# A new order of tasks and choice of engines for an adaLN block with linear attention

## The chip, the cores and the metric

The kernel runs on one core of a Trainium2 chip. The metric is the device time of one execution in microseconds (us); lower is better. Times quoted from the profile belong to one profiled execution of the kernel before the change. Its engines are called by short names: PE multiplies matrices, DVE, ACT and POOL work on vectors, and SP only issues DMAs.

## The reference

One transformer block over a sequence of 2048 tokens of width 512, in bfloat16. A vector `c` gives six vectors of scale, shift and gate. The attention is linear: queries and keys go through a small matrix per head (32 heads of 16), and two softmaxes (of the result and of its negative) make a feature map of 32.

```python
mod = (silu(c) @ w_mod).reshape(6, 512)          # sa, ca, ga, sb, cb, gb
h = layernorm(x) * (1 + ca) + sa
q, k, v = h @ wqkv                               # 32 heads x 16
phi_q = concat(softmax(q @ w_phi), softmax(-q @ w_phi))
phi_k = concat(softmax(k @ w_phi), softmax(-k @ w_phi))
kv, z = sum_s(phi_k[s] v[s]), sum_s(phi_k[s])    # over all 2048 tokens
x = x + ga * ((phi_q @ kv) / (phi_q @ z + 1e-6)) @ wo
h = layernorm(x) * (1 + cb) + sb
x = x + gb * ((sigmoid(h @ w_gate) * (h @ w_up)) @ w_down)      # width 1376
```

## The kernel before

The tokens are cut into 16 tiles of 128, and each step on a tile (or on a piece of one) is a *task*: a name, the engines that can do it, a function that issues its instructions, the tasks it depends on and the buffers it uses. A table `ORDER` (lines 39 to 91), one long text of task names, sets everything else. `arrange` walks it once:

```python
for word in text.split():
    name, _, e = word.partition("@")
    t = self.tasks[name]
    t.eng = LETTER[e] if e else next(iter(t.alts))
    assert t.eng in t.alts and t.deps <= done and t not in done, name
    for b in t.bufs:
        if b.slot is None:
            b.slot = slots[b.cls].pop(0)
```

So a name's place in the table sets its place in its engine's program (each engine runs its instructions in order), a suffix `@A`, `@D` or `@P` puts it on ACT, DVE or POOL, and buffers are handed out in the table's order from a fixed number per class; the one that became free first is taken first. Exponentials, feature maps and the like share a class of seven. A task waits by semaphore for its inputs and for the last readers of the buffer that it takes over. Nothing else is scheduled.

The first stage runs until the key-value sum is complete:

- `ld_*` on SP load 256-KB pieces of x (`x0b` is tiles 2-3, `x0a` tiles 0-1, L537), the key weights (`wk0`, `wk1`, L545), the scale and shift weights (`wm00a` to `wm01b`, four pieces, L542), then the value weights (L551), the gate's and the second block's modulation weights (`wmga`, L555; `wmm2`, 1.5 MB, L556), `wo` (L557) and the MLP's weights. DMA transposes on the same queue serve query weights (L669) and tiles 10 to 13 (`xT1`, L736).
- `st1` (L702, L703), `rs1` (POOL L712, L713 or ACT L709, L710), `nmr1` (L718) and `xn1` (L731) are the first layer norm; PE transposes the tiles (`tph`, L744) and `hm1` (L753 on DVE and POOL, L751 on ACT) applies scale and shift, which `modc1` on PE (L630) and `modc1c` (ACT L635, L636 or DVE L638) have put into columns.
- PE: folding of `w_phi` into the weights, then `K` (L817), `V` (L821), `Q` (L871). `warm` (L600) are 18 filler matmuls at the beginning.
- Per tile: `e` and `qe`, exponentials on ACT (L776); `n` and `qn`, sums on DVE (L780); `r`, reciprocals (DVE L798 or ACT L794, L795); `phi` of keys (L787) and `qphi` of queries (L784), the products exponential by reciprocal, on DVE or POOL:

```python
engine(e).tensor_tensor(ph[:, a * P:b * P].rearrange(...), ee[:, a:b].rearrange(...), kr[:, a:b]..., op=ALU.mult)
...
port=("POOL", "DVE"))
```

  A tile's feature map may be cut into halves or quarters (`phi13.0` and `phi13.4`; `phi11.0` to `phi11.6`).
- `kv` on PE (L282) adds every tile's feature map times values; `kvn` and `kvz` on DVE (L294, L299) mask the sum into `kvb`.

Behind it PE does `num` (L326, queries by `kvb`), `out` (L356), and the MLP (`g`, `u` at L447, `y` at L485), with DVE, ACT and POOL serving it. `wo` (L851) and `wd` (L860) on POOL multiply the gates into the weights.

Of the kernel before, what the change touches and what calls it, by code (L numbers as in the profile page):

```python
# [15 lines left out]
P = 128  # L16
S, D, H, DH, F = 2048, 512, 32, 16, 1376
# [23 lines left out]
nmr1_1 nmr1_2 ld_x1b st1_6 st1_7 tpw1 tpw3 wTc3 wTc1 tpw2 fold10 foldc10 wTc2 ld_wm00b ld_x1a ld_wm00a tph00 fold11 fold13 rs1_4 foldc13 fold12 foldc12 xn1_3  # L41
xn1_2 xn1_1 modc1.0 tph10 tph11 st1_4 tph20 tph01 ld_x2b foldc11 tph22 warm1_5 modc1c0 hm1_11@A nmr1_4 xn1_6 xn1_7 st1_5 rs1_3@P st1_11 st1_10 warm1_6
hm1_20@A hm1_10@A tph21 warm1_7 tph41 tph42 hm1_21 rs1_6@P nmr1_3 tph13 ld_wm01a ld_wm01b modc1.1 hm1_01@A hm1_00@A hm1_41@A tph03 tph23 K2a ld_x2a tph02
modc1c1 st1_8 ld_x3a warm1_8 K1a hm1_23 xn1_5 xn1_4 tph12 nmr1_6 st1_9 hm1_03@A hm1_13@A hm1_02@A ld_wv0 wqT3 xn1_10 xn1_11 rs1_5@P K0a K0b tph31 hm1_42@A
warm1_9 hm1_12@A hm1_22@A tph32 e0.0 K3a tph30 K3b hm1_30@A ld_wmga K1b tph33 warm1_10 tph40 st1_14 st1_15 st1_13 hm1_31@A hm1_32 wqT0 e3.0 wqT1 K2b hm1_40
nmr1_5 rs1_8@P n0.0 nmr1_8 hm1_33 e2.0 V0a V1a fold03 xn1_9 xn1_8 V1b V0b e1.0 n2.0 V2a V2b tph50 hm1_50 warm1_11 xn1_15 xn1_14 n1.0 V3a wqT2 fold00 fold01
tph43 r0.0@A va1 va0 phi0.0 foldc03 fold02 foldc01 foldc02 n3.0 st1_12 foldc00 xT1_10 xT1_11 r2.0 va2@D ld_wmm2 modca.0 modca.1 hm1_60@P hm1_63@P hm1_62@P
tph82 hm1_82@A r3.0@A modcac r1.0@A phi2.0@D phi1.0@D V3b K4a K4b rs1_7@P Q0 Q2 kv0.0 Q1 qe0.0 va3 qe2.0 hm1_43@A qe1.0 modc2.0 tph52 modc2.1 tph51 nmr1_7
xn1_12 xn1_13 phi3.0@D ld_wo qn0.0 modc2c e4.0 kv1.0 qn2.0 hm1_52 kv2.0 Q4 K5a kv3.0 xT1_12 xT1_13 qphi0.0@P qphi0.1@P qn1.0 qe4.0 qphi2.1 tph80 K5b hm1_80@A
hm1_51@A e5.0 pT0 qphi2.0 n4.0 r4.0@A qn4.0 n5.0 phi4.0@D qphi1.1@P hm1_61@P qphi1.0@P tph53 V5 K7a V4 va5 hm1_53@A V6 pT2 hm1_70@P qphi4.1 va4 hm1_71 mask4  # L50
va6 K6a K7b K6b e6.0 K8 tph83 hm1_83 r5.0 qphi4.0@P e8.0 pT1 pT4 ld_wd2 tph81 hm1_81 n6.0 n8.0 e7.0 n7.0 V7 kv4.0 hm1_72@P K11 K9 V9 K14 V8 r6.0@A e9.0 va7
va9 r7.0@A e11.2 e11.6 phi5.0 phi6.0 hm1_73@P n9.0 r9.0@A kv5.0 gwa gra gwb e11.4 e14.0 K10 phi7.0@D kv6.0 K12 V10 kv7.0 e14.4 r8.0 n11.6 n11.2 r11.6 phi9.0
e10.0 e12.0 ld_wd ld_wu0 grb n11.4 n14.0 r11.2 n14.4 r14.0 n10.0 r14.4@A phi8.0 va8 V11 V14 n12.0 e11.0 K13 n11.0 phi11.6 r11.4 wo1 r11.0 va10 r10.0@A va11
kv8.0 kv9.0 phi11.2@D phi11.0@D phi10.0@D phi11.4@D V12 K15 e13.0 wmod_free ld_wg0 phi14.4 phi14.0 kv10.0 kv11.4 kv11.6 Q6 kv11.0 e13.4 r12.0@A e15.4 n13.0
n13.4 r13.0 r13.4 n15.4 e15.0 va14 V15 V13 qe6.0 va12 kv11.2 n15.0 r15.0 r15.4@A va13 phi13.4 Q5 phi15.4 phi13.0@D va15 phi15.0@D phi12.0@D wo0 wo3 Q3 kv12.0
# [4 lines left out]
hm0.4 hm0.9 u0.2 u0.0 num6a tg0.5 tg0.0 rd3a u3a u0.5 g0.2 hm0.0 hm0.5 rd6a nmr2_1 qe10.0 tg0.2 oT4 g0.10 u0.10 wd6 hm0.2 g0.3 pT7 tg0.3 u6a g0.6 num6b u0.3  # L60
y0.0 y0.1 rd6b tg0.10 hm0.10 hm0.3 num5a num5b u6b rd5b wd3 wd4 wd5 oT3 oT6 xn2_1 qe13.0 tg0.6 rd5a y0.2 u5b g0.7 tg0.7 out4 u5a oT5 qn11.0 u0.6 u0.7 xnT1
num7a hm0.6 hm0.7 mod13@A mod12@A rd7a x1_4 y0.3 out3 qphi11.1@P qphi11.0@P x1_3 st2_3 out6 mod10@A mod11@A g1.2 tg1.2 g1.1 tg1.1 num7b wd7 u1.3 u1.2 hm1.2
u7a g1.4 u1.1 y0.4 rd7b hm1.1 u1.4 y0.5 tg1.4 hm1.4 g1.0 g1.10 u1.10 g1.3 u7b st2_2 rs2_2 tg1.10 tg1.3 hm1.10 hm1.3 pT11 out5 tg1.0 u1.7 g1.7 x1_6 nmr2_2 u1.0
hm1.0 g1.5 u1.5 x1_5 qn10.0 wd8 y0.6 g1.6 oT7 xn2_2 xn2_3 g1.8 y0.7 Q14 y0.8 wd10 tg1.7 tg1.5 hm1.5 out7 u1.8 u1.6 st2_4 tg1.6 xnT2 xnT3 wd9 x1_7 qphi10.0 Q12
hm1.7 st2_6 mod21@P mod20@P qphi10.1@P y1.0 pT10 tg1.8 mod22@A mod23@A hm1.6 g1.9 y1.1 y1.2 tg1.9 u1.9 y0.9 y1.3 y1.4 g2.5 y0.10 g2.6 st2_5 qe12.0 st2_7 hm1.8
qn9.0 tg2.5 qe14.0 rs2_4 hm1.9 rs2_3 nmr2_4 y1.5 u2.0 g2.1 g2.0 tg2.0 xn2_7@D hm2.0 nmr2_3 fin0 y1.6 g2.2 tg2.2 u2.6 u2.2 hm2.2 u2.1 num11b y1.7 g2.4 rd11b
u11b xn2_6@P xnT7 xnT6 u2.5 tg2.1 xn2_5 qphi9.1@P hm2.1 tg2.6 u2.8 xn2_4 hm2.5 g2.3 num11a rd11a u11a u2.9 qphi9.0@P xnT5 y1.8 xnT4 tg2.4 u2.4 hm2.4 hm2.6
# [991 lines left out]
```

## Time and profile before

| | before |
|---|---|
| median of 3 runs | 205.57 us (205.29 to 205.62) |
| profiled execution: span | 203.3 us |
| what lies around the span, against the median | 2.27 us |
| PE busy | 194.9 us (96%) |
| DVE busy | 160.6 us (79%) |
| ACT busy | 105.9 us (52%) |
| POOL busy | 102.1 us (50%) |
| DMA | 22.94 MB in 49,453 packets |

The profile gives no time of its own for the profiled execution but its span. Busy shares are means over two very different stages: until about 58 us all of PE, DVE, ACT and POOL work, and behind that PE is the busiest by far. An engine's busy time counts its fillers too (PE's `warm`). Idle time of an engine is listed with what released it.

### The profile page before, as it was taken

To read this page: it belongs to the slowest core of one execution; us is meant where nothing else is said; L and a number is where in the kernel's file an instruction comes from. 1 tells how busy PE (TensorE), PEld (TensorE's weight loads), DVE (VectorE), ACT (ScalarE), POOL (GpSimd) and SP (SyncE) were. 2 spreads that over 40 slices of the span, in tenths; PEclk is the share of its full clock that TensorE was granted. 3 is DMA by queue.
4 is the path that set the end of the run, shared out by engine and by line. 5 is a ranking of instruction groups with operands and counts; after the bars stand their busy time and mean duration, and the time that the engine had idled before them with its cause. 6 is when DMAs were issued, how large, how long until landed. Compare 5 with 4: busy or idle time off the path is not lost.

```text
span 203.3 us, 4138 instructions
## 1 busy us (share of the span) xinstructions
PE 194.9 (96%) x1447; PEld 106.7 (52%) x1471; DVE 160.6 (79%) x374; ACT 105.9 (52%) x257; POOL 102.1 (50%) x143
## 2 busy tenths in 40 slices
PE   7789999999999999999999999999999999999993
PEld 2455655555464687668844444444444444444442
DVE  3899999999999999999897797794969844326633
ACT  2799999999978984556451115212113311324100
POOL 4698977789689999767670056230030324000000
PEclk9999999999999999999999999999999999999999
DMA  5999975669952792417637224433112030100111
GB/s 172 331 329 182 233 264 102 123 82 280 400 213 43 146 102 55 94 37 106 125 59 103 51 54 103 101 83 77 26 26 69 13 79 31 40 13 7 50 55 55
DMA packets 49453, 22.94 MB, mean 113 GB/s; under 512 B 38065, under 2 KB 47634, under 8 KB 49426
## 3 DMA queue, kind: packets, MB, share of 16 engines
q1 hardware_dynamic: 48896, 22.59, 48.6%
q8 instruction: 13, 0.21, 0.4%
q14 instruction: 14, 0.11, 0.2%
q10 hardware_dynamic: 530, 0.02, 0.1%
HBM read 11.58 MB, written 2.10 MB: 67 GB/s over the span
## 4 chain that ended last, share of the span: by engine, by line
PE 75%; DVE 8%; ACT 4%; DMA 4%; issue 4%; POOL 3%; SPq 0%; POOLq 0%; DVEq 0%
PE y_ps L485 19%; PE u_ps L447 18%; PE g_ps L447 17%; PE a_ps L356 5%; DMA wmod_sb<-in_w_mod_dram 4%; PE k_ps L817 3%; PE warm L600 3%; DVE ks L780 3%; PE num L326 2%; POOL phi L787 2%; PE q_ps L871 2%; PE v_ps L821 2%; PE g_ps L449 1%; ACT h1T L751 1%; DVE qks L780 1%
## 5 line engine op out<-in xcount | busy, mean ns | idle before, releaser
L457 ACT ACTIVATE tg<-g_ps 128x512 bf16<-128x512 f32 (+5 forms) x66 | 28.8, 455 | 66.7 <-PE g_ps L447 39.5
L468 DVE SCALAR_TENSOR_TENSOR wmod_sb<-tg,u_ps 128x512 bf16<-128x512 bf16 (+4 forms) x63 | 30.3, 492 | 18.0 <-ACT tg L457 11.3
L485 PE MATMUL y_ps<-wd_sb,wmod_sb 128*128 128x512 bf16 (+4 forms) x180 | 44.2, 366 | 0.2
L447 PEld LDWEIGHTS <-wg_sb 128*128 128x128 bf16 (+1 forms) x252 | 21.9, 99 | 16.1 <-issue 0.2
L447 PEld LDWEIGHTS <-wu_sb 128*128 128x128 bf16 (+1 forms) x252 | 21.8, 99 | 16.0 <-issue 0.3
L784 POOL TENSOR_TENSOR qphi<-qe,qks 128x512 bf16<-128x512 bf16 x24 | 25.1, 1063 | 3.9 <-DMA pT<-qphi 1.0
L485 PEld LDWEIGHTS <-wmod_sb 128*128 128x128 bf16 (+1 forms) x187 | 17.1, 98 | 16.0 <-issue 0.6
L447 PE MATMUL u_ps<-wT_sb,wu_sb 128*128 128x512 bf16 (+2 forms) x124 | 23.8, 322 | 0.1
L447 PE MATMUL g_ps<-wT_sb,wg_sb 128*128 128x512 bf16 (+2 forms) x122 | 23.0, 321 | 0.2
L447 PE MATMUL g_ps<-wqk_sb,wg_sb 128*128 128x128 bf16 (+4 forms) x127 | 19.9, 286 | 0.1
L447 PE MATMUL u_ps<-wqk_sb,wu_sb 128*128 128x128 bf16 (+4 forms) x127 | 19.8, 286 | 0.2
L492 DVE TENSOR_TENSOR ot<-y_ps,x 128x512 bf16<-128x512 f32 (+2 forms) x17 | 11.1, 654 | 10.5 <-PE y_ps L485 10.4
L780 DVE TENSOR_REDUCE qks<-qe 128x64 bf16<-128x1024 bf16 x16 | 19.2, 1204 | 0.0
L780 DVE TENSOR_REDUCE ks<-e 128x64 f32<-128x1024 bf16 (+2 forms) x22 | 19.1, 905 | 0.0
L376 POOL TENSOR_SCALAR ve<-mv 128x2 f32<-128x2 f32 (+1 forms) x8 | 1.8, 226 | 34.2 <-DVE mv L366 34.1
L776 ACT ACTIVATE e<-k_ps 128x512 bf16<-128x512 f32 (+2 forms) x44 | 17.7, 504 | 0.1
L776 ACT ACTIVATE qe<-q_ps 128x512 bf16<-128x512 f32 x32 | 17.3, 608 | 0.8 <-POOL phi L787 0.4
L787 POOL TENSOR_TENSOR phi<-e,kr 128x1024 bf16<-128x1024 bf16 (+2 forms) x10 | 14.5, 1454 | 3.9 <-ACT kr L795 2.1
L817 PE MATMUL k_ps<-wqk_f,h1T 128*128 128x512 bf16 x61 | 15.9, 379 | 0.1
L356 PE MATMUL a_ps<-wo_sb,oT 128*128 128x512 bf16 x60 | 15.9, 379 | 0.2
L871 PE MATMUL q_ps<-wqk_f,h1T 128*128 128x512 bf16 x60 | 15.7, 379 | 0.2
L821 PE MATMUL v_ps<-wv_sb,h1T 128*128 128x512 bf16 x62 | 15.5, 379 | 0.0
(131 smaller groups left out, 306.4 us busy)
## 6 DMA issues: line engine op xcount, KB each, us to landing
out_dram<-ot SPq DMA_DIRECT2D x15, 128.0 KB, 1.8
x_sb<-in_A_x_dram SPq DMA_DIRECT2D x6, 256.0 KB, 4.9
wmod_sb<-in_w_mod_dram SPq DMA_DIRECT2D x1, 1536.0 KB, 7.4
wu_sb<-in_B_w_up_dram SPq DMA_DIRECT2D x1, 1376.0 KB, 11.0
wg_sb<-in_B_w_gate_dram SPq DMA_DIRECT2D x1, 1376.0 KB, 10.4
wd_sb<-in_B_w_down_dram SPq DMA_DIRECT2D x1, 1280.0 KB, 8.0
wmod_sb<-in_w_mod_dram SPq DMA_DIRECT2D x4, 256.0 KB, 6.0
wqk_sb<-in_A_wqkv_dram SPq DMA_DIRECT2D x2, 256.0 KB, 4.5
```

The lines of the kernel that those rows point to most:

```text
L356: pe.matmul(ap_[:], lhsT=oT[:, j, :], rhs=wo_sb[:, j, :], start=(j == 0), stop=(j == KT - 1))
L447: pe.matmul(ps[:fsz, 0:n], lhsT=w[:, j, ft * P:ft * P + fsz], rhs=h[:, j, 0:n], start=(j == 0), stop=(j == KT - 1))
L457: G.add(f"tg{k}.{ft}", {"ACT": 0.13 + n * 0.00083}, lambda e, tg=tg, g_ps=g_ps, fsz=fsz, n=n: act.activation(tg[:fsz, 0:n], g_ps[:fsz, 0:n ...
L468: dve.scalar_tensor_tensor(hm_all[:fsz, hm[k].slot, ft, 0:n], tg[:fsz, 0:n], 1.0, u_ps[:fsz, 0:n], op0=ALU.add, op1=ALU.mult)
L485: mm = pe.matmul(y[:, 0:c1 - c0], lhsT=hm_all[:fsz, hm[k].slot, ft, tl * P:(tl + 1) * P], rhs=wd_sb[:fsz, ft, c0:c1], start=(ft == 0), sto ...
L776: act.activation(ee[:, a:b, s].rearrange("p g f h -> p g (f h)"), kp[:, a * 64:b * 64].rearrange("p (g n) -> p g n", n=64), ACT.Exp, scale ...
L780: dve.tensor_reduce(ks[:, a:b].rearrange("p g s h -> p (g s) h"), ee[:, a:b].rearrange("p g s f h -> p (g s) h f"), axis=AX.X, op=ALU.add)
L784: engine(e).tensor_tensor(ph[:].rearrange("p (g s f h) -> p g s f h", s=2, f=DH, h=4)[:, :, s], ee[:, :, s], ks[:, :, 1 - s].unsqueeze(2). ...
L787: engine(e).tensor_tensor(ph[:, a * P:b * P].rearrange("p (g f h) -> p g f h", f=DH, h=4), ee[:, a:b].rearrange("p g s f h -> p (g s) f h" ...
L817: pe.matmul(kp[:], lhsT=h1T[:, j, t * P:(t + 1) * P], rhs=wqk_f[:, j, D:2 * D], start=(j == 0), stop=(j == KT - 1))
L821: pe.matmul(vp[:], lhsT=h1T[:, j, t * P:(t + 1) * P], rhs=wv_sb[:, j, :], start=(j == 0), stop=(j == KT - 1))
L871: pe.matmul(qp[:], lhsT=h1T[:, j, t * P:(t + 1) * P], rhs=wqk_f[:, j, 0:D], start=(j == 0), stop=(j == KT - 1))
```

## The change

Only the table `ORDER` is replaced. All task names stay; their order and some engine suffixes change. A line or two of it:

```diff
-pmem ld_x0b wdz warm0 c1 warm1_0 warm1_1 bd st1_2 st1_3 warm1_2 warm1_3 c2 rs1_2 ld_x0a ld_wk0 warm1_4 tpw0 st1_0 rs1_0 wTc0 st1_1 ld_wk1 rs1_1 c3 xn1_0
+wdz warm0 c1 warm1_0 warm1_1 ld_x0b mask4 ld_wk0 c2 ld_x0a st1_3 tpw0 warm1_2 tpw1 wTc0 warm1_3 ld_wk1 warm1_4 warm1_5 warm1_6 wTc1 st1_2 rs1_2 warm1_7 pmem
...
```

On SP, at the program's beginning before the change (L537 are x tiles, L545 key weights, L542 scale and shift weights; two rows alike in a row are counted):

```order
L537 DMA x_sb<-in_A_x_dram 128x2x512 x2
L545 DMA wqk_sb<-in_A_wqkv_dram 128x2x512 x2
L537 DMA x_sb<-in_A_x_dram 128x2x512
L542 DMA wmod_sb<-in_w_mod_dram 128x4x256
L537 DMA x_sb<-in_A_x_dram 128x2x512
L542 DMA wmod_sb<-in_w_mod_dram 128x4x256
L537 DMA x_sb<-in_A_x_dram 128x2x512
L542 DMA wmod_sb<-in_w_mod_dram 128x4x256 x2
L537 DMA x_sb<-in_A_x_dram 128x2x512
```

The same place of SP after it:

```order
L537 DMA x_sb<-in_A_x_dram 128x2x512
L545 DMA wqk_sb<-in_A_wqkv_dram 128x2x512
L537 DMA x_sb<-in_A_x_dram 128x2x512
L545 DMA wqk_sb<-in_A_wqkv_dram 128x2x512
L542 DMA wmod_sb<-in_w_mod_dram 128x4x256
L537 DMA x_sb<-in_A_x_dram 128x2x512
L542 DMA wmod_sb<-in_w_mod_dram 128x4x256
L537 DMA x_sb<-in_A_x_dram 128x2x512
L542 DMA wmod_sb<-in_w_mod_dram 128x4x256 x2
L537 DMA x_sb<-in_A_x_dram 128x2x512
```

The first half of the key weights now stands between the first two loads of x, and the last two of the scale and shift weights stand ahead of the first load of the third pair of x tiles (tiles 8 and 9). Later on SP, the two transposes of tiles 10 and 11 (L736) stood ahead of the 1.5 MB of modulation weights (L556) and `wo` (L557), and stand behind them now.

On POOL, from phi5.0 (the first row; `phi` is L787) to the `wo` pieces behind the last feature map of the first stage (phi15.4), before:

```order
L787 TENSOR_TENSOR phi<-e,kr 128x1024 x2
L753 TENSOR_SCALAR h1T<-h1T,modc 128x256
L787 TENSOR_TENSOR phi<-e,kr 128x1024 x2
L787 TENSOR_TENSOR phi<-e,kr 128x256
L851 TENSOR_TENSOR wo_sb<-wo_sb,ga_sb 128x512
L787 TENSOR_TENSOR phi<-e,kr 128x512 x4
L851 TENSOR_TENSOR wo_sb<-wo_sb,ga_sb 128x512 x3
```

And the same place of POOL after:

```order
L787 TENSOR_TENSOR phi<-e,kr 128x1024
L753 TENSOR_SCALAR h1T<-h1T,modc 128x256
L851 TENSOR_TENSOR wo_sb<-wo_sb,ga_sb 128x512
L787 TENSOR_TENSOR phi<-e,kr 128x1024 x3
L787 TENSOR_TENSOR phi<-e,kr 128x256 x4
L851 TENSOR_TENSOR wo_sb<-wo_sb,ga_sb 128x512
L787 TENSOR_TENSOR phi<-e,kr 128x512 x4
L851 TENSOR_TENSOR wo_sb<-wo_sb,ga_sb 128x512 x2
```

POOL gets all four quarters of tile 11 instead of one, and one more `wo` piece ahead of the four halves of tiles 13, 14 and 15.

On DVE, from the reciprocals of tile 11 to the mask of the key-value sum (`kvb`), before:

```order
L798 RECIPROCAL kr<-ks 128x16 x2
L787 TENSOR_TENSOR phi<-e,kr 128x256 x2
L787 TENSOR_TENSOR phi<-e,kr 128x1024
L787 TENSOR_TENSOR phi<-e,kr 128x256
L780 TENSOR_REDUCE ks<-e 128x32 x2
L798 RECIPROCAL kr<-ks 128x32 x2
L780 TENSOR_REDUCE ks<-e 128x32 x2
L798 RECIPROCAL kr<-ks 128x32
L787 TENSOR_TENSOR phi<-e,kr 128x512 x2
L787 TENSOR_TENSOR phi<-e,kr 128x1024
L780 TENSOR_REDUCE qks<-qe 128x64
L294 TENSOR_TENSOR kvb<-kvacc_595,mask_77 128x16x16
```

The end of the same stretch after (its earlier part is `n` and `r` in another order, without the three quarters of tile 11):

```order
L787 TENSOR_TENSOR phi<-e,kr 128x1024
L780 TENSOR_REDUCE ks<-e 128x32
L798 RECIPROCAL kr<-ks 128x64
L798 RECIPROCAL kr<-ks 128x32
L780 TENSOR_REDUCE ks<-e 128x32
L787 TENSOR_TENSOR phi<-e,kr 128x1024
L780 TENSOR_REDUCE ks<-e 128x32 x2
L798 RECIPROCAL kr<-ks 128x32 x3
L787 TENSOR_TENSOR phi<-e,kr 128x512 x2
L780 TENSOR_REDUCE qks<-qe 128x64
L299 SCALAR_TENSOR_TENSOR kvb<-kvacc_685,mask_77 128x16
L294 TENSOR_TENSOR kvb<-kvacc_685,mask_77 128x16x16
```

DVE has the reciprocals of tile 12 and of the second half of tile 15 from ACT, and no longer the three quarters of tile 11. Further ahead (not shown), the mask's own reduction (L591) moves from the place behind a `qphi` in the middle of the stage to the second instruction of DVE, four `hm1` leave DVE and one of half size comes to it, two modulation columns (L638) come to it from ACT, and two rsqrt pairs (`rs1_4` from ACT, and `rs1_7` from further back) stand ahead of phi0.0 on POOL. Behind `kvb` the order of the MLP's pieces changes throughout; the work of the last tile pair ends the program as before.

More of the change, by code (lines that the diff above doesn't have):

```diff
@@ L44 @@
[L44 to L55, printed above, removed]
@@ L60 @@
[L60 to L67, printed above, removed]
@@ new lines @@
+r3.0@A modc2.1 nmr1_7 xn1_13 xT1_13 hm1_60@P modc2c Q0 phi2.0@D kv0.0 hm1_62@P xn1_12 xT1_12 phi1.0@D qn4.0 kv1.0 qe0.0 qe1.0 hm1_80@A kv2.0 V6 Q2 phi3.0@D
+qn0.0 qphi4.1@P va6 kv3.0 qphi4.0@P qn1.0 qe2.0 pT4 qphi0.0 qphi0.1@P hm1_63@P e4.0 K7a qphi1.0@P hm1_70@P qphi1.1 hm1_61@P qn2.0 K6a tph81 K7b qphi2.0@P K6b
+V8 n4.0 e5.0 va8 hm1_73@P V4 n5.0 hm1_71@P e6.0 pT0 pT1 K9 r4.0@A va4 V5 va5 K8 qphi2.1 r5.0 K11 phi4.0@D kv4.0 V7 phi5.0 hm1_72@P n6.0 e7.0 pT2 e9.0 wo1 e8.0
+hm1_81@A e11.4 K10 n7.0 va7 e11.6 n9.0 kv5.0 r6.0 V9 r9.0 n8.0 K14 r7.0@A phi7.0@D V11 phi6.0 e11.0 n11.0 n11.6 e11.2 n11.2 n11.4 K13 kv6.0 kv7.0 r8.0 phi9.0
@@ L87 @@
+y14.9 fin12 y14.10 fin14 y15.4 st12 st14 y15.5 y15.6 y13.4 y13.5 y13.6 y13.7 y13.8 y13.9 y13.10 fin13 st13 y15.7 y15.8 y15.9 y15.10 fin15 y15.0b y15.1b st15
+y15.2b y15.3b y15.4b y15.5b y15.6b y15.7b y15.8b y15.9b y15.10b fin15b st15b
 """
```

66 lines of the change are left out of this document (40 added, 26 removed).

## The prediction

> **What bounds the kernel now.** I first read the busy time of each engine in five stretches of the span (columns: stretch, its length, then busy us and instructions of PE, PEld, DVE, ACT and POOL, the granted clock, the DMA share and GB/s).
>
> ```profile
> core 0: us, PE busy (x) PEld busy (x) DVE busy (x) ACT busy (x) POOL busy (x), PEclk, DMA share, GB/s
> 0.00:10.00 10.00, 7.47 (x46) 3.53 (x47) 6.12 (x21) 5.36 (x13) 5.22 (x23) 1.00 0.85 250
> 10.00:20.00 10.00, 9.23 (x89) 5.29 (x90) 9.45 (x32) 9.86 (x28) 9.07 (x17) 1.00 1.26 256
> 20.00:57.90 37.90, 37.36 (x355) 21.02 (x360) 37.05 (x67) 36.47 (x103) 30.43 (x32) 1.00 0.83 222
> 57.90:103.40 45.50, 44.62 (x465) 32.01 (x469) 42.76 (x119) 31.60 (x77) 38.43 (x45) 1.00 0.50 86
> 103.40:203.30 99.90, 96.17 (x502) 44.87 (x510) 65.25 (x140) 22.65 (x39) 19.00 (x30) 1.00 0.25 55
> ```
>
> Behind 57.9 us PE alone is dense: 140.8 of 145.4 us. Ahead of it PE is busy too, but part of that is warming and its real work is not what ends the stage: PE, DVE and ACT are all nearly full from 20 to 57.9 us, and POOL is the one with air, 7.5 us idle of 37.9. What ends the stage is seen at its last step, in the timeline of POOL, DVE and PE around 57 us (start, length, engine, line, operation, tiles, idle time before it and its releaser).
>
> ```profile
> 56.48 1.20 POOL L787 TENSOR_TENSOR phi<-e,kr 128x512 bf16<-128x512 bf16 x1 [1.23 <-ACT kr L795]
> 55.47 1.29 DVE L787 TENSOR_TENSOR phi<-e,kr 128x512 bf16<-128x512 bf16 x3
> 57.87 0.43 DVE L294 TENSOR_TENSOR kvb<-kvacc,mask 128x256 bf16<-128x256 f32 x1
> 58.57 0.80 PE L326 MATMUL num<-kvb,pT 128*128 128x68 bf16 x20 [0.36 <-DVE kvb L299]
> ```
>
> The key-value sum needs the feature map `phi` of every one of the 16 token tiles. POOL's last one (phi15.4) ends at 57.68, PE adds it, DVE masks the sum at 57.87 (`kvb`), and PE starts `num` at 58.57 after waiting. So kvb is a gate between two stages: whatever moves it moves everything behind, because behind it PE has nearly no slack to give back (0.9 us in the first 45.5). The question is when kvb comes in the new order, and both DVE and POOL must be through their lists for it.
>
> **The change, step 1: DVE's head.** DVE's waits up to 58 us are few (waiting instruction, what it waited for, total us, times, longest).
>
> ```profile
> DVE st L702 <- DMA x_sb<-in_A_x_dram: 2.4, 1, 2.4
> DVE h1T L753 <- PE tp_h L744: 0.6, 2, 0.4
> DVE phi L787 <- POOL h1T L753: 0.3, 1, 0.3
> DVE nmr L718 <- ACT rs L710: 0.3, 1, 0.3
> ```
>
> SP now issues x tiles 2-3, half the key weights, then x tiles 0-1; before, both x pairs went first. The issues of those loads today, with the time to landing of each, and the statistics of the first tile of the second pair:
>
> ```profile
> x_sb<-in_A_x_dram SPq DMA_DIRECT2D x1, 256.0 KB, 2.8
> x_sb<-in_A_x_dram SPq DMA_DIRECT2D x1, 256.0 KB, 3.1
> wqk_sb<-in_A_wqkv_dram SPq DMA_DIRECT2D x1, 256.0 KB, 4.4
> 5.21 0.66 DVE L702 BATCH_NORM_STATS2 st<-x_sb 128x6 f32<-128x512 bf16 x1
> ```
>
> They are issued about 0.5 us apart (0.9, 1.5 and 2.0 us in the trace); the third lands at about 6.3. If x tiles 0-1 take the third place they land there, and DVE, ready for them at 5.21, waits 1.1 us. The other end is no wait at all, if place does not matter and this load keeps 3.1 us. I take 1.1, because queue and size are those of the third row. Against it: the mask reduction (0.28 us, L591) moves from a full place at 38 us into DVE's first wait, where it is free (-0.28); the `nmr` wait (0.3) and the two `h1T` waits (0.6) can go, as their instructions stand further back now. Head together: 1.1 - 0.28 - 0.9 = about -0.1.
>
> The last two scale-and-shift loads (L542) move ahead of the first load of tiles 8-11, so they come one place of 256 KB earlier, and those tiles one place later. What the former release, the last columns of scale and shift, comes from PE, and PE's list ahead of `num` holds the same amount of real work as before and does not set the gate; the statistics of tiles 8-11 stand behind others in DVE's list. I cost this at nothing; its cover is DVE and ACT, 9.45 and 9.86 us busy of the 10 from 10 to 20 us. Without that cover it is worth at most a place in the queue, about 0.5 us by the distance of the issues, either way.
>
> **Step 2: DVE's list up to phi7.0.** Mean durations by shape up to 57.8 us (count | busy us, mean ns):
>
> ```profile
> L787 DVE TENSOR_TENSOR phi<-e,kr 128x1024 bf16<-128x1024 bf16 x7 | 4.7, 682 | 0.3 <-POOL h1T L753 0.3
> L753 DVE TENSOR_SCALAR h1T<-tp_h,modc 128x256 bf16<-128x256 bf16 x9 | 3.5, 393 | 0.6 <-PE tp_h L744 0.6
> L798 DVE RECIPROCAL kr<-ks 128x64 bf16<-128x64 f32 x3 | 1.6, 538 | 0.0
> L784 DVE TENSOR_TENSOR qphi<-qe,qks 128x512 bf16<-128x512 bf16 x3 | 1.4, 478 | 0.0
> L798 DVE RECIPROCAL kr<-ks 128x16 bf16<-128x16 f32 x4 | 0.9, 234 | 0.0
> L787 DVE TENSOR_TENSOR phi<-e,kr 128x512 bf16<-128x512 bf16 x2 | 0.7, 388 | 0.0
> 44.58 0.69 DVE L787 TENSOR_TENSOR phi<-e,kr 128x1024 bf16<-128x1024 bf16 x1 [0.29 <-POOL h1T L753]
> ```
>
> Ahead of the phi of tile 7 DVE loses four `hm1` (1.57) and gains one of half size (0.39 at most), loses two `qphi` and gains two, gains two reciprocals (1.08) and two small modulation columns (0.23 each at most, the shortest reciprocal). Net +0.3 at most; I take +0.2. phi7.0 ends at 45.27 today, so at 45.27 + 0.2 - 0.1 = about 45.4.
>
> **Step 3: POOL behind phi7.0.** POOL's timeline of today from there on, and its mean durations by shape from 18 to 57.8 us:
>
> ```profile
> 45.42 4.61 POOL L787 TENSOR_TENSOR phi<-e,kr 128x1024 bf16<-128x1024 bf16 x3 [0.87 <-ACT kr L795]
> 49.99 1.17 POOL L851 TENSOR_TENSOR wo_sb<-wo_sb,ga_sb 128x512 bf16<-128x512 bf16 x1
> 52.19 3.06 POOL L787 TENSOR_TENSOR phi<-e,kr 128x512 bf16<-128x512 bf16 x3 [1.03 <-DVE phi L787]
> ```
>
> ```profile
> L787 POOL TENSOR_TENSOR phi<-e,kr 128x1024 bf16<-128x1024 bf16 x5 | 9.6, 1917 | 1.6 <-ACT kr L795 0.9 <-PE kvacc L282 0.5
> L851 POOL TENSOR_TENSOR wo_sb<-wo_sb,ga_sb 128x512 bf16<-128x512 bf16 x2 | 2.3, 1164 | 0.0
> L787 POOL TENSOR_TENSOR phi<-e,kr 128x256 bf16<-128x256 bf16 x1 | 0.6, 619 | 0.1
> ```
>
> Today POOL starts phi9.0 at 45.42 and ends phi15.4 at 57.68: 12.3 us, of which 2.3 are the two waits shown. In the new table phi9.0 writes into the buffer that phi7.0 has read out, so it starts just behind it again, at about 45.5. From there to phi15.4 POOL now has two phi of 1.92, four quarters of tile 11 at 0.62 (three of them were DVE's), one `wo` piece of 1.16 and four halves of 1.02: 3.8 + 2.5 + 1.2 + 4.1 = 11.6, less a little overlap at the seams: 11.5 us without a wait. DVE in return loses three of those short phi (under 0.39 each, the mean of a half tile) and a reciprocal and gets two that ACT had (0.54 each at most): even. POOL gets to phi9.0 in time: from phi0.0 to there it loses two `qphi` and gains two, and gains one `hm1` (1.64 us for three today, shown below) and one `wo` piece, 1.7 us net, out of 7.5 - 2.3 = 5.2 us of idle time; another rsqrt pair now comes ahead of phi0.0.
>
> **Step 4: DVE and POOL at the same time.** In the trace a two-operand product of DVE out of SBUF hardly ever runs beside one of POOL: POOL mostly waits just then. In the few places where they meet, this is what it costs (two qphi of DVE, the first beside POOL's second, which ends at 33.05; then a qphi of POOL beside one of DVE's that ends at 38.10, and one alone).
>
> ```profile
> 30.98 2.07 POOL L784 TENSOR_TENSOR qphi<-qe,qks 128x512 bf16<-128x512 bf16 x2 [0.55 <-PE kvacc L282]
> 32.73 0.60 DVE L784 TENSOR_TENSOR qphi<-qe,qks 128x512 bf16<-128x512 bf16 x1
> 33.25 0.41 DVE L784 TENSOR_TENSOR qphi<-qe,qks 128x512 bf16<-128x512 bf16 x1
> 37.68 0.42 DVE L784 TENSOR_TENSOR qphi<-qe,qks 128x512 bf16<-128x512 bf16 x1
> 37.79 1.22 POOL L784 TENSOR_TENSOR qphi<-qe,qks 128x512 bf16<-128x512 bf16 x1 [0.82 <-DVE phi L787]
> 35.37 1.06 POOL L784 TENSOR_TENSOR qphi<-qe,qks 128x512 bf16<-128x512 bf16 x1
> ```
>
> DVE lost 0.19 us of 0.32 us side by side, POOL 0.16 of 0.31, and phi15.4 above 0.15 (1.20 against 1.05) of 0.28: about half of the time they share. With POOL dense in the new order the gaps are gone. Behind phi7.0 DVE has two phi of 0.68 and two of 0.39, 2.1 us; if three quarters of that lie beside POOL's work, half of it is 0.8 us on POOL. Ahead of phi7.0 DVE's products come in five groups; five times 0.16 by three quarters is 0.6 us on DVE. [...]
>
> [...]
>
> **The sum.** Start of phi9.0 45.5 (with DVE's 0.6 later: 46.1), 11.5 of POOL, 0.8 for sharing, 0.2 from phi15.4's end to kvb (57.68 to 57.87): 58.6. DVE's own list agrees: what it has ahead of kvb in the whole stage sums up the same as before, so 57.87 - 0.1 + 0.6 + its share behind phi7.0 is about 58.5. kvb comes 0.7 us later, the rest follows at its length. The profiled span is 203.3 and the median 205.57, so 2.27 us lie around the span; I add 0.7 to the median: 206.3.
>
> **The rivals.** (1) *Faster: POOL's wait goes and nothing is lost.* If x tiles 0-1 land by 5.2 us, the head gains 1.2 instead of 0.1 (its waits of 0.9 and the mask's 0.28), and if DVE's products still fall between POOL's, step 4 is nothing. DVE's list then ends 1.0 us earlier, POOL's at 44.4 + 11.5 + 0.2, earlier still; kvb at 56.9, time 204.6. For it: POOL has enough idle time in sum, and two of POOL's waits of today (1.23 and 1.03) have no place in the new list. Against it: the 4.4 us of the third load, and 11.5 us without a gap. 0.29.
>
> (2) *No change:* x tiles 0-1 wait 0.55 instead of 1.1, so kvb moves by 0.15, or the sharing costs half of my 1.4 us, and 0.7 - 0.7 is nothing; either is inside 0.4 us of today. About 0.2% (0.4 us) is what a measurement of this kernel can tell from no change. 0.12.
>
> [...] A late end would also come if POOL, which runs in order, had to wait for the DMA transposes of tiles 10-11 (two on SP's queue today ahead of 2 MB of weights, now behind them):
>
> ```profile
> wmod_sb<-in_w_mod_dram SPq DMA_DIRECT2D x1, 1536.0 KB, 7.4
> 18.12 3.23 SPq L736 DMA_TRANSPOSE h1T<-xn  x2
> 24.88 1.64 POOL L753 TENSOR_SCALAR h1T<-h1T,modc 128x256 bf16<-128x256 bf16 x3
> ```
>
> If the 1.5 MB are issued at the transposes' old place, 18.1, they land at 25.5 and the transposes some 2 us behind them; POOL wanted them at 24.88 today and comes to them later in the new list, by two rsqrt pairs and an `xn`. So this costs 1 us or less, inside the range. 0.14.
>
> (4) *The forecast*, 0.45, own range 206.0 to 207.2.
>
> **The numbers.** Faster 0.29, within 0.2% 0.12, slower 0.45 + 0.14 = 0.59. The range goes from 204.6, rounded down to 204.5, to 208.2: it leaves out the lower half of (1) and the upper half of (3).
>
> **What would show it.** Right: POOL dense from phi9.0 to phi15.4 with its phi of 1.92 and 1.05 grown, DVE's products grown or preceded by gaps, DVE's second pair of statistics waiting for x, kvb between 58.3 and 59. Wrong: kvb ahead of 57.5 with DVE's and POOL's products at today's durations (rival 1); DVE's products near 1 us or more (rival 3); POOL idle at 29 us for the transposes; or a changed time with kvb where it was, which would mean that PE's list behind the gate, which I hold equal, is what changed.

## The result and the profile after

The changed kernel takes 212.56 us (median of 4 runs, 211.71 to 212.94) against 205.59 for the kernel before: ratio 1.033, 95% interval 1.029 to 1.037. It is slower by 7 us, where 0.7 was forecast. Its profiled execution took 212.8 us with a span of 210.9, so 1.9 us lie around the span.

The busy time of the engines in the same first four stretches of the changed kernel (columns as before):

```profile
0.00:10.00 10.00, 8.76 (x71) 4.86 (x72) 6.26 (x20) 5.60 (x14) 5.70 (x24) 1.00 0.87 249
10.00:20.00 10.00, 9.20 (x76) 5.30 (x74) 8.20 (x27) 9.02 (x22) 7.92 (x15) 0.83 1.24 267
20.00:57.90 37.90, 35.29 (x324) 18.97 (x328) 37.76 (x63) 34.27 (x93) 35.28 (x38) 1.00 0.80 227
57.90:103.40 45.50, 41.79 (x445) 28.71 (x447) 41.90 (x119) 29.41 (x73) 38.36 (x44) 1.00 0.39 71
```

Three things differ. POOL is nearly full from 20 to 57.9 us (35.3 instead of 30.4) and yet the stage is not over at 57.9. PE's clock was 0.83 of full speed in the second stretch. And PE has 3.7 us idle in the fourth, where it had 0.9. The gate itself, in the timelines of DVE and PE:

```profile
62.07 0.41 DVE L294 TENSOR_TENSOR kvb<-kvacc,mask 128x256 bf16<-128x256 f32 x1
62.53 1.08 PE L326 MATMUL num<-kvb,pT 128*128 128x68 bf16 x28 [0.98 <-DVE kvb L294]
```

`num` starts at 62.53 instead of 58.57, 4.0 us late; from there the program takes 210.9 - 62.5 = 148.4 us instead of 203.3 - 58.6 = 144.7, another 3.6. These two make up the 7.6 us by which the span grew. The clock differs between the two profiles (a mean of 0.992 here, 1.000 before); a profile of the changed kernel at full clock comes further down.

**Ahead of the gate** the grown pieces are DVE's products. Its groups up to 61.9 us:

```profile
L787 DVE TENSOR_TENSOR phi<-e,kr 128x1024 bf16<-128x1024 bf16 x7 | 6.1, 884 | 0.0
L784 DVE TENSOR_TENSOR qphi<-qe,qks 128x512 bf16<-128x512 bf16 x3 | 3.0, 1035 | 0.0
L787 DVE TENSOR_TENSOR phi<-e,kr 128x512 bf16<-128x512 bf16 x2 | 1.6, 834 | 0.0
```

The same twelve products took 4.7, 1.4 and 0.7 us before; they take 3.9 us more. Seven of them end late, behind a piece of POOL that was running when they began; the other five take 0.40 to 0.71 us, about as before. Two of them beside POOL, first DVE's row, then POOL's:

```profile
46.80 1.21 DVE L787 TENSOR_TENSOR phi<-e,kr 128x1024 bf16<-128x1024 bf16 x1
45.55 1.91 POOL L787 TENSOR_TENSOR phi<-e,kr 128x1024 bf16<-128x1024 bf16 x1
...
56.12 1.42 DVE L787 TENSOR_TENSOR phi<-e,kr 128x1024 bf16<-128x1024 bf16 x1
55.95 1.05 POOL L787 TENSOR_TENSOR phi<-e,kr 128x512 bf16<-128x512 bf16 x1
56.96 1.50 POOL L787 TENSOR_TENSOR phi<-e,kr 128x512 bf16<-128x512 bf16 x1
```

POOL's piece ends at 47.46; DVE's product, issued at 46.80, ends at 48.01, 0.55 behind it. In the second pair DVE ends 0.54 behind POOL's first piece (57.00), and POOL's next piece, begun at 56.96, takes 1.50 instead of 1.05. That is no sharing by halves: the 0.66 us that the first product spends beside POOL's piece cost it 0.53 (against 0.68 for a product alone), the 0.88 of the second cost 0.74, and the 0.58 that POOL's last piece spends beside DVE cost that one 0.45. So each side stands still while the other's piece runs, but for 0.13 or 0.14 us in these pairs; I call this the lock. DVE's waits make little of the delay:

```profile
DVE st L702 <- DMA x_sb<-in_A_x_dram: 2.2, 2, 1.9
DVE h1T L753 <- PE tp_h L744: 1.3, 1, 1.3
DVE wd_sb L593 <- PEq L1043: 0.9, 1, 0.9
DVE vaug L836 <- PE v_ps L821: 0.3, 1, 0.3
DVE mask L591 <- POOL ident masks.py:199: 0.2, 1, 0.2
```

They sum to 4.9 us, against 4.5 before (the four rows shown ahead of the result, and the same 0.9 for the fillers' weights).

**Behind the gate** PE's waits:

```profile
PE num L326 <- DMA pT<-qphi: 1.3, 1, 1.3
PE num L326 <- DVE kvb L294: 1.0, 1, 1.0
PE num L326 <- DVE qphi L784: 0.6, 1, 0.6
PE a_ps L356 <- DMA oT<-o: 0.3, 1, 0.3
```

The kernel before had only the wait for kvb there. The 1.3 and 0.6 us are `num` of tiles 11 and 12, at 98.55 and 116.64 us. The new table puts tile 11's close behind the transpose of the query features (`pT`) that it reads. The second is put down to `qphi` in this profile; in the full-clock profile of the same kernel both (1.3 and 0.7 us) are put down to `pT`.

### The profile page after: what moved, and what is told of

The parts are those of the page before. It is cut to its first block, busy times and chain, and to the rows that moved or that the text cites. A ratio compares the mean times of both kernels' runs of the same rounds, so it can differ in the third digit from the quotient of the medians.

```text
span 210.9 us, 4154 instructions
## 1 busy us (share of the span) xinstructions
PE 197.7 (94%) x1448; PEld 106.8 (51%) x1471; DVE 163.7 (78%) x373; ACT 107.4 (51%) x250; POOL 107.1 (51%) x146
## 4 chain that ended last, share of the span: by engine, by line
PE 65%; DVE 12%; ACT 6%; issue 6%; POOL 5%; DMA 4%; DVEq 0%; POOLq 0%
PE u_ps L447 15%; PE y_ps L485 14%; PE g_ps L447 14%; PE a_ps L356 5%; PE q_ps L871 3%; PE k_ps L817 3%; DVE ks L780 2%; DVE phi L787 2%; ACT e L776 2%; DMA pT<-qphi 2%; POOL qphi L784 2%; DVE qks L780 2%; PE warm L600 2%; DMA oT<-o 2%; PE num L326 2%
## 5 line engine op out<-in xcount | busy, mean ns | idle before, releaser
L485 PE MATMUL y_ps<-wd_sb,wmod_sb 128*128 128x512 bf16 (+4 forms) x183 | 43.1, 366 | 0.1
L784 POOL TENSOR_TENSOR qphi<-qe,qks 128x512 bf16<-128x512 bf16 x26 | 27.4, 1074 | 4.8 <-DVE qks L780 3.8
L447 PE MATMUL g_ps<-wT_sb,wg_sb 128*128 128x512 bf16 (+2 forms) x122 | 23.5, 321 | 0.3
L776 ACT ACTIVATE e<-k_ps 128x512 bf16<-128x512 f32 (+2 forms) x44 | 18.4, 501 | 1.5 <-POOL qphi L784 1.2
L817 PE MATMUL k_ps<-wqk_f,h1T 128*128 128x512 bf16 x61 | 17.5, 404 | 1.3 <-ACT e L776 1.0
L787 POOL TENSOR_TENSOR phi<-e,kr 128x1024 bf16<-128x1024 bf16 (+2 forms) x13 | 16.9, 1318 | 1.0 <-DVE phi L787 0.6
L361 DVE TENSOR_TENSOR x<-a_ps,x_sb 128x512 f32<-128x512 f32 x16 | 10.8, 685 | 5.5 <-PE a_ps L356 5.4
```

Source lines behind the costliest of these rows:

```text
L447: pe.matmul(ps[:fsz, 0:n], lhsT=w[:, j, ft * P:ft * P + fsz], rhs=h[:, j, 0:n], start=(j == 0), stop=(j == KT - 1))
L485: mm = pe.matmul(y[:, 0:c1 - c0], lhsT=hm_all[:fsz, hm[k].slot, ft, tl * P:(tl + 1) * P], rhs=wd_sb[:fsz, ft, c0:c1], start=(ft == 0), sto ...
L776: act.activation(ee[:, a:b, s].rearrange("p g f h -> p g (f h)"), kp[:, a * 64:b * 64].rearrange("p (g n) -> p g n", n=64), ACT.Exp, scale ...
L784: engine(e).tensor_tensor(ph[:].rearrange("p (g s f h) -> p g s f h", s=2, f=DH, h=4)[:, :, s], ee[:, :, s], ks[:, :, 1 - s].unsqueeze(2). ...
L787: engine(e).tensor_tensor(ph[:, a * P:b * P].rearrange("p (g f h) -> p g f h", f=DH, h=4), ee[:, a:b].rearrange("p g s f h -> p (g s) f h" ...
L817: pe.matmul(kp[:], lhsT=h1T[:, j, t * P:(t + 1) * P], rhs=wqk_f[:, j, D:2 * D], start=(j == 0), stop=(j == KT - 1))
```

## The experiments

All are edits of one of the two tables, or of the functions that issue POOL's and DVE's work. Where a kernel writes constants instead of values, or leaves a factor out, its expectation says so.

**Which stage.** The table of one kernel up to the second mask of the sum (`kvn1`), the rest in the other's order.

```diff
 # e1: ORDER of before through kvn1, then every other task in the order of after
 # e2: ORDER of after through kvn1, then every other task in the order of before
```

> The table of before up to the second mask of the key-value sum, then every remaining task in the order of after. Theory (two causes: a lock between DVE's and POOL's products ahead of the gate, about 4 us, and PE waits of the new order behind it, about 2.6 us): the gate is back at 57.9 us, the waits behind it stay, 207.5 to 209.0 us. Rival A (the new order behind the gate is fine and only suffers from the late gate): 205.2 to 206.0. Rival B (the tail is most of the loss): above 210.

> The table of after up to the second mask of the key-value sum, then every remaining task in the order of before. Theory: the gate stays at 62 us and the rest runs as before, 209.0 to 210.2 us. Rival A (a late gate costs more behind it, whatever the order there): 212 to 213. Rival B (the tail is most of the loss): below 207.5.

Measured: old gate with new tail 209.99 us (ratio 1.021, 1.017 to 1.026), new gate with old tail 210.31 (1.022, 1.017 to 1.027). The first is 1.0 us above the theory's range, the second 0.1. Each half alone costs nearly 5 us. In the first, part of it comes from the joint: `num` waited 1.2 us for query exponentials that the new order has ahead of the gate, so 4.7 us is too much for the tail. The second is the cleaner one: `num` started at 61.97 and the program ended 145.5 us later, 0.8 more than before and 2.8 less than with the new tail.

**The lock.** POOL as long busy, but without reading: its products read 4 elements and fill the output by memsets.

```diff
+if e == "POOL":
+    pool.tensor_tensor(o4[:, a, s, 0, :], ee[:, a, s, 0, :], ..., op=ALU.mult)
+    pool.memset(ph[:, a * P:b * P], 0.03125)        # qphi: its half of ph
+    pool.memset(...)                                # e3: the same again; e5: cut to the product's length
```

> The table of after; POOL's key and query products read only 4 elements each and then fill their output by two memsets of about the same length together, so POOL is as long busy but reads nothing (the products' values are left out). Theory (the two engines lock each other out only where both read SBUF): DVE's products beside POOL's fall from 0.88 and 1.04 us to 0.7 and 0.45, kvb comes at 58.0 to 59.0 instead of 62.1, time 208 to 209.5. Rival A (POOL's list is too long by itself, DVE's products grow with any work of POOL): kvb at 61 or later, 211.5 to 213.

> As the run before in which POOL's products wrote without reading, but with the second memset cut so that one product with its small read and its memsets is as long as the product it stands for (1.9, 1.05, 1.0 and 0.6 us); the products' values are left out. Theory (the lock acts only while POOL reads SBUF): beside memsets DVE's products take 0.68 and 0.42 us, only those beside hm1, xn or wo pieces stay long; kvb at 58.5 to 60 instead of 62.1, 209 to 210.5 us. Rival (POOL's list is too long for the stage, whatever it does): kvb at 61.5 or later, 211.5 to 213 us.

The first took 217.46 us (1.057, 1.051 to 1.063), a miss for both theories: with two full memsets and the small read the pieces had become longer than the products, and PE waited 4.9 us for POOL's key features. The second has them at length: 209.21 us (1.019, 1.013 to 1.024). That is 3.4 us below the changed kernel by the medians, but three of its four runs had a full clock (209.19 us in the median), and the changed kernel's two such runs took 211.08 and 211.94: at equal clock it is about 2.3 us below. Its DVE groups up to 59 us:

```profile
L794 DVE TENSOR_TENSOR phi<-e,kr 128x1024 bf16<-128x1024 bf16 x7 | 4.9, 714 | 0.2 <-DMA pT<-qphi 0.2
L791 DVE TENSOR_TENSOR qphi<-qe,qks 128x512 bf16<-128x512 bf16 x3 | 1.5, 501 | 0.4 <-DMA pT<-qphi 0.3
L794 DVE TENSOR_TENSOR phi<-e,kr 128x512 bf16<-128x512 bf16 x2 | 0.8, 422 | 0.0
```

The gate, and a pair of DVE and POOL, in its timeline:

```profile
58.63 0.42 DVE L294 TENSOR_TENSOR kvb<-kvacc,mask 128x256 bf16<-128x256 f32 x1
...
45.22 0.68 DVE L794 TENSOR_TENSOR phi<-e,kr 128x1024 bf16<-128x1024 bf16 x1
44.79 0.95 POOL L786 MEMSET phi<- 128x1024 bf16 x1
45.80 0.74 POOL L789 MEMSET phi<- 128x768 bf16 x1
```

Same order, same work on DVE, POOL as busy (35.3 us of the 37.9 from 20 to 57.9 us in both): the products fall back to 7.2 us in sum and the gate to 58.6, from 62.1 in the profile above and 60.0 at full clock. A product of DVE beside a memset of POOL takes 0.68 us, as alone, and the memset is not longer either (0.95, the mean of its size in the run before). So it is POOL's reading that matters here: 1.21 and 1.42 us beside its products, 0.68 beside its memset.

What remained beside `hm1`, `xn` and `wo` pieces was taken away in a further kernel, in which these write memsets too.

```diff
+pool.tensor_scalar(dst[:, 0:4], src[:, 0:4], ...); pool.memset(dst, 0.03125)   # hm1, xn, wo alike
```

> The table of after; besides POOL's products, its hm1, xn and wo pieces also read only 4 elements and then fill their output by memsets of about their length (values left out). Theory (the lock makes the gate late): DVE's products at 0.68 and 0.42 us throughout, kvb at 57.5 to 58.3, 207.8 to 209 us, what remains being the waits behind the gate. Rival (POOL's list or the head makes at least 2 of the 4 us): kvb at 59.5 or later, 210 or more.

It took 211.33 us (1.028, 1.023 to 1.033), with kvb at 59.65: what the rival had said, and a miss of the theory. The products are at 4.7, 1.3 and 0.8 us, the 6.8 of the kernel before, so the lock is gone; but PE waits 0.7 us for POOL's last key features. A small read with its memset was longer than the piece it stood for where that was not blocked (0.93 us in the mean instead of 0.76 for `xn`, 0.69 instead of 0.55 for `hm1`), and without the lock POOL's list is the next to be late. It gives the price of the lock on DVE (10.7 - 6.8 = 3.9 us), not a clean price in time.

DVE's side: a constant instead of the second input.

```diff
-engine(e).tensor_tensor(ph[...], ee[...], kr[...].to_broadcast(...), op=ALU.mult)
+dve.tensor_scalar(ph[...], ee[...], 0.25, None, op0=ALU.mult)      # on DVE only
```

> The table of after; DVE's products take one input from SBUF and a constant instead of two inputs (the factor by the reciprocal is left out there). Theory (it is the second SBUF input of DVE that needs what POOL holds): DVE's products take 0.7 us or less and 0.45 or less beside POOL's, kvb at 57.5 to 58.7, 208 to 209.3 us. Rival A (any fast bf16 operation of DVE out of SBUF is locked out): products stay at 0.88 and 1.04 in the mean, 212 to 213 us.

Measured 207.94 us (1.013, 1.007 to 1.018), with the gate at 57.40: both just below the theory's ranges. But not for its reason:

```profile
43.95 0.97 DVE L786 TENSOR_SCALAR phi<-e 128x1024 bf16<-128x1024 bf16 x1
42.72 1.92 POOL L791 TENSOR_TENSOR phi<-e,kr 128x1024 bf16<-128x1024 bf16 x1
55.79 0.47 DVE L786 TENSOR_SCALAR phi<-e 128x512 bf16<-128x512 bf16 x2
57.40 0.41 DVE L294 TENSOR_TENSOR kvb<-kvacc,mask 128x256 bf16<-128x256 f32 x1
```

The one-input form is blocked as well: issued at 43.95, it ends at 44.92, 0.28 behind POOL's piece. It gains because it is shorter (two halves in 0.47 us, where the two-input halves of the kernel before take 0.39 each). The theory that the second input alone does it fell.

**One part of the change in the old table.** Three quarters of tile 11 to POOL.

```diff
-phi11.2@D ... phi11.0@D ... phi11.4@D
+phi11.2@P ... phi11.0@P ... phi11.4@P
```

> The table of before with one part of the change alone: three quarters of tile 11's key features go from DVE to POOL. Without a lock POOL has 2.3 us of waits to take its 1.9 us and DVE is relieved of 0.8: kvb at 57.1 to 57.6, 204.7 to 205.3 us. With the lock POOL runs without a gap beside DVE's four products that follow, each side waits for the other: kvb at 58.7 to 59.3, 206.2 to 206.9 us.

206.43 us (1.005, 1.001 to 1.008), kvb at 59.1: the values forecast with the lock, but only in part by its path. The lock shows: DVE's half of tile 13 took 0.93 us beside POOL's piece of tile 13 (the mean of a half was 0.388), and the first of POOL's quarters took 1.06 us beside a DVE product, instead of 0.62. But POOL did not run without a gap:

```profile
51.45 5.24 POOL L787 TENSOR_TENSOR phi<-e,kr 128x256 bf16<-128x256 bf16 x6
57.79 1.05 POOL L787 TENSOR_TENSOR phi<-e,kr 128x512 bf16<-128x512 bf16 x1 [1.11 <-ACT kr L795]
```

Its last piece waited 1.11 us for ACT's reciprocal, and ahead of that ACT's exponentials had waited 0.4 and 0.3 us for feature maps of POOL, from which they take over buffers. The chain that ended last goes from POOL's quarters (to 53.67) through PE's `kv` and the matmuls between them to kvb, and 0.34 of the 1.27 us by which kvb is late was there before tile 11. So this run does not separate the lock from the length of POOL's list.

**The head.** The old table up to e0.0, then the new one; and the part of the change that its description names, alone.

```diff
 # e7: ORDER of before through e0.0, then every other task in the order of after
 # e8, in the table of before:
-... ld_x2b ... ld_wm01a ld_wm01b ... ld_x2a
+... ld_wm01a ld_wm01b ld_x2b ... ld_x2a
```

> The table of before up to its first exponential (e0.0, about 17 us), then every remaining task in the order of after. Theory (the lock in the middle is the cause of the late gate, the new head costs at most the 1.3 us that DVE waits for PE's transposes at the halved clock): kvb at 60.5 to 62, 211 to 212.7 us. Rival (the head with its clock at 0.5 from 13 to 16 us sets the whole delay): kvb at 58 to 59, 208 to 209 us.

> The table of before with one change: the last two loads of scale and shift weights stand ahead of the first load of tiles 8 and 9. Theory (the named part of the change is worth nothing here, DVE and ACT are full and these loads do not set the gate): 205.0 to 205.8 us. Rival A (the columns come earlier and shorten the head): 204.4 to 204.9. Rival B (the statistics of tiles 8 to 11 come late and DVE waits for them): 206 to 206.6.

The first took 215.99 us (1.049, 1.044 to 1.055), a miss on all sides: the old head does not serve the new rest, and DVE waited 2.5 us for PE's transposes. So it shows nothing of how much of the delay the head sets. The second took 206.69 (1.004, 1.001 to 1.008), above the ranges of all three theories, and its ten runs fall apart by the granted clock: 205.51, 204.93 and 205.71 where it was full, 206.67 to 207.81 in six where the mean was 0.983. In its profile:

```profile
10.00:20.00 10.00, 8.99 (x74) 4.94 (x73) 8.57 (x27) 8.37 (x23) 8.82 (x15) 0.66 1.24 279
```

So with a full clock the loads are worth nothing that can be told. The low clock came in six of ten runs here and in two of 13 of the kernel before on the same chip; of all 60 runs of the kernel before in these experiments, 14 had 0.983 (median 206.81) and 22 a full clock (205.15). That the loads bring the low clock about is not shown.

**The changed kernel again**, on the chip of the last runs.

> The changed kernel itself, for runs on the same chip as the next ones, with their granted clocks: 211 to 213 us; runs at a clock of 0.997 or more, if there are any, about 1 us below those at 0.992.

212.69 us (1.035, 1.031 to 1.038). Two of six runs had a full clock, 211.08 and 211.94; with the first four, eight of ten are near 0.99, with a median of 212.8. The clock costs this order 1.3 us (212.8 against 211.5, the median of the two). The profile of a run with full clock has DVE's waits up to 60 us, and the gate in its timeline, without that cost:

```profile
DVE st L702 <- DMA x_sb<-in_A_x_dram: 1.9, 1, 1.9
DVE wd_sb L593 <- PEq L1043: 0.9, 1, 0.9
DVE mask L591 <- POOL ident masks.py:199: 0.2, 1, 0.2
```

```profile
60.00 0.41 DVE L294 TENSOR_TENSOR kvb<-kvacc,mask 128x256 bf16<-128x256 f32 x1
```

DVE waits 3.0 us instead of 4.5: the head is better by 1.5 us. Its products still take 6.1, 3.0 and 1.6. So the gate is 2.1 us late: 3.9 for the lock less 1.5 for the head, within 0.3. The head's gain is not steady, though. Three other profiles with this order ahead of the gate and a clock of 0.997 or more (e2, e6 and e9) have the start of `num`, 60.46 here and 58.57 before, at

```profile
61.97 0.41 PE L326 MATMUL num<-kvb,pT 128*128 128x68 bf16 x8 [0.98 <-DVE kvb L294]
61.35 1.08 PE L326 MATMUL num<-kvb,pT 128*128 128x68 bf16 x28 [0.98 <-DVE kvb L294]
60.86 1.08 PE L326 MATMUL num<-kvb,pT 128*128 128x68 bf16 x28 [0.98 <-DVE kvb L294]
```

DVE waits 2.2 to 3.3 us for x there instead of 1.9, and in two of them 0.9 and 1.0 us for a `qphi` of POOL. So at full clock the gate is 1.9 to 3.4 us late.

**Behind the gate.** Moves of `num`, in the table of after.

```diff
 # e6: num10a num10b rd10a u10a behind y1.5; num12a num12b rd12a u12a behind u3.2
 # e9: num11b num11a behind g2.0; num12a num12b rd12a u12a behind u3.2
 # e15: e9's moves with e14's writes
```

> The table of after with two moves behind the gate: num of tile 10 (with its reciprocal and its first division) a few y pieces later, num of tile 12 behind four more matmuls of u. Theory (at these two places PE waits 1.3 and 0.6 us for DMA transposes of the query features that stand right ahead of num in the table): 210.5 to 211.3 us. Rival (DVE or ACT run in order behind and take the time back): 212 to 213 us.

> The table of after with num of tile 11 moved behind five groups of g and u, and num of tile 12 behind four groups as before. In the run that moved num of tiles 10 and 12, the 1.3 us gap stayed: it stands between Q of tile 12 and u of the third unit, which is num of tile 11. Theory (PE had nothing between the transpose of tile 11's query features and their use): that gap goes and 1.3 us with it or most of it, 210.7 to 211.6 us. Rival (DVE's reciprocals of num stand in order ahead of work that PE needs, so the wait moves to the next u): 212 to 212.6.

> As all_pool_writes, with num of tiles 11 and 12 moved back as in the run before. Theory (lock at the gate plus waits for the query features' transposes are the whole loss but for some tenths): 206.3 to 207.5 us. Rival (a third cause of 2 us or more is left): above 208.3.

The first was 212.17 us (1.032, 1.027 to 1.037): I had moved the wrong tile, the 1.3 us stayed. The second, with tile 11, was 211.03 (1.028, 1.022 to 1.034), 210.35 at full clock. PE's waits then:

```profile
PE a_ps L356 <- DVE den L329: 0.6, 1, 0.6
PE num L326 <- DMA pT<-qphi: 0.3, 1, 0.3
PE y_ps L485 <- DVE o L333: 0.3, 1, 0.3
PE g_ps L447 <- DVE o L333: 0.2, 1, 0.2
```

The 1.3 us is gone; of the wait at tile 12 (0.6) half is left and two small ones behind it take the rest. The third was 211.01 us (1.025, 1.020 to 1.030), 0.3 below the same kernel without the moves, since a new wait of 1.4 us for a transpose came elsewhere. It missed the forecast, so the two causes do not simply add up in it.

> The table of before up to the first y of the third unit (about 120 us), then the remaining tasks in the order of after. Theory (the new order loses nothing in the last third): 205 to 205.9 us. Rival (the new end costs 0.5 us or more by itself): 206 to 206.8.

213.15 us (1.038, 1.033 to 1.042), a miss that tells nothing of the end of the new order: at the joint `num` waited 3.5 us for a transpose that the new table has elsewhere.

**A version of the old table** with small gains that the profile offered: the mask in DVE's first wait, and three fillers where PE waits at 8 us.

```diff
-... mask4 (in the middle) ...
+wdz mask4 ...
 # e12 as well: three warm1 ahead of fold10, three fewer behind
```

> The table of before with the mask's reduction (0.28 us) in DVE's first wait for x instead of the middle of the stage. Theory (DVE has no slack ahead of the gate): 0.2 to 0.3 us faster, 205.05 to 205.2. Rival (POOL's last feature map sets the gate, DVE waits for it): no change, 205.3 to 205.4.

> As the run with the mask first, and three of the filler matmuls stand ahead of the first folding matmul, where PE waits 0.9 us for ACT, instead of at 16 to 22 us. Theory (the halved clock follows an idle PE between 8 and 12 us): runs with a granted clock under 0.995 get fewer, fastest runs as in the run with the mask first, median 204.7 to 205.1. Rival (the fillers later on are what keeps the clock): more of such runs, median above 205.5.

205.64 us (1.001, 0.997 to 1.004) and 206.02 (1.001, 0.998 to 1.005): no gain that can be told. Ten of twelve runs with the mask first and eight of twelve with the fillers early were below the full clock, where it was 19 of 29 for the kernel before on the same chip. No version here beats the kernel before.

## Why the prediction was wrong, point by point

**What bounds** was right: kvb is the gate, DVE and POOL must both be through, and what comes late there stays late. All runs with a late kvb are late at the end.

**Step 1**, the head: too dear by about 0.8 us. x tiles 0-1 in the third place landed 3.6 to 3.8 us after their issue, not 4.4, and DVE waited 0.3 us, not 1.1; in one profile with a full clock all of rival 1's gain in the head came (1.5 us, 1.2 forecast), in three others 0.1 to 1.2.

**Steps 2 and 3**, the lists, held: POOL's work fitted in time, DVE's sum was even.

**Step 4 failed.** It is the term that was mis-sized: 0.6 us on DVE and 0.8 on POOL, by half of the shared time; measured, 3.9 us on DVE's products alone. On POOL the sum was about right: from phi9.0 to the end of phi15.4 it took 12.6 us (48.09 to 60.65), where 11.5 and 0.8 were forecast. So DVE's list, and not POOL's, ended last. The rows quoted there already spoke for the lock: DVE's `qphi` ended 0.28 us behind POOL's piece, just as every blocked product of that size does after (0.28 to 0.29). I read 0.19 lost of 0.32 as a rate; it was a full stop less a start of 0.13, as in the pairs above, and only because the three meetings were short did the two look alike. Rival 3, whose chance of 0.14 was for a slower end, is the lock: a price of 2.2 us over the forecast, or 208.5, was worked out for it, and the upper end of the range goes by that. No run shows this price; in its place the runs show the 3.9 us. I had five entries of DVE waiting half a piece of 1.06 in three quarters of the cases, where seven products waited, and the pieces are up to 1.92 long.

**"The rest follows at its length" failed too**: 3.6 us. I had checked that PE's work ahead of the gate stays the same and took its order behind it as dense. Two `num` stand there behind their own transposes; 1.3 + 0.6 us are shown by their waits, 1.3 of it by moving tile 11. PE's waits shown for that stretch sum to 2.2 us behind kvb. Of the other 1.4, about 1.0 is busy time of PE (141.5 instead of 140.5 us for the same matmuls); why it grew is open.

**What I had not on the list**: the clock. PE has gaps from 10 to 12.8 us, and then the clock falls; in single microseconds of the changed kernel:

```profile
10.00:11.00 1.00, 0.77 (x15) 0.52 (x12) 0.96 (x4) 1.00 (x4) 0.88 (x3) 1.00 1.17 304
11.00:12.00 1.00, 0.58 (x5) 0.33 (x5) 0.96 (x4) 1.00 (x4) 0.54 (x1) 1.00 1.57 238
...
14.00:15.00 1.00, 1.00 (x4) 0.31 (x3) 0.96 (x3) 0.91 (x3) 0.92 (x3) 0.50 1.15 315
15.00:16.00 1.00, 1.00 (x7) 0.72 (x6) 0.60 (x4) 0.34 (x1) 0.92 (x3) 0.50 1.12 335
16.00:17.00 1.00, 1.00 (x12) 0.61 (x10) 0.08 (x1) 0.77 (x3) 1.00 (x3) 0.87 1.10 332
```

The clock is halved for about 3.4 us (all of 13 to 16 us and, by the means of 0.93 and 0.87, 0.4 of the two microseconds around it), PE's transposes come late and DVE stands for 1.3 us (its busy share in the last row is 0.08). That it is these gaps is not shown, and two profiles speak against gaps alone. In the full-clock profile of the changed kernel PE is busy for 0.79, 0.65 and 0.86 of the microseconds from 9 to 12; and the kernel before, at full clock, has

```profile
8.00:9.00 1.00, 0.08 (x2) 0.08 (x3) 0.99 (x4) 1.00 (x3) 0.42 (x1) 1.00 1.18 315
9.00:10.00 1.00, 0.65 (x10) 0.47 (x11) 0.94 (x4) 0.84 (x2) 1.00 (x2) 1.00 1.12 321
11.00:12.00 1.00, 0.63 (x7) 0.39 (x7) 0.96 (x4) 1.00 (x5) 1.00 (x2) 1.00 1.15 311
```

The one experiment that moved fillers made no clear difference. So the cause of the clock's fall is open; its price is measured (1.3 us).

By size, in the profiled run: 3.9 us for the lock on DVE and 0.4 more waiting at the head (1.9 that the run at full clock has not, 1.3 of it for PE's transposes, less the 1.5 that the head gained there) against 4.0 at the gate, and 3.6 behind it. At full clock the changed kernel is 6.4 us slower (211.5 against 205.15). Taking away the reading of POOL's products gave back 2.3 of them. That is less than the 3.5 us by which DVE's products shrank, since DVE's waits ahead of the gate sum to 5.0 us in that run's profile, where the changed kernel has 3.0 at full clock. In the same profile `num` starts 0.5 us later than before and the rest takes 3.6 us longer than before.

## What to carry to other kernels

Where two engines lock each other out, as DVE's products and POOL's do here (0.53 us lost of 0.66 side by side), put their reading pieces in turn (not tried here), and look what the idle time of the one is for: in six of POOL's eight waits of 0.5 us or more from 24 us to the old gate a product of DVE ran undisturbed, so most of its 7.5 us was no room. A short overlap cannot tell a shared rate from a lock with a fixed start (0.19 us lost of 0.32 before, 0.74 of 0.88 after); look at when the blocked piece ends against the other's end. And an order that moves work ahead of a gate must be followed past it: a consumer right behind its own DMA transpose makes its engine wait for what is left of the transpose, 1.3 us here.

## What the runs showed of the hardware

- DVE's product of two SBUF inputs ends 0.54 to 0.55 us (1024 columns) behind the end of the POOL piece that blocks it (0.28 to 0.29 with 512), where it takes 0.62 to 0.71 when nothing blocks it; POOL's piece behind it grows from 1.05 to 1.50. Beside a memset of POOL neither grows (0.68, 0.95).
- DVE's tensor-scalar out of SBUF in bf16 is blocked like that (0.97 us, ending 0.28 behind POOL's piece, where the seven of its size take 0.65 in the mean).
- PE's clock fell to 0.5 behind 3 us in which PE was still busy for three quarters of the time (0.77, 0.58 and 0.85 of three microseconds), in some runs and not in others (a mean of 0.992 in the first profile of the changed kernel, 0.999 in the second). It stayed there for about 3.4 us; in the profile of e8, with a mean of 0.983, for twice as long (about 11.6 to 18.4 us).
